# Two heads' attention products in one batch, float32 cluster scores with their split on GpSimd, and a shorter buffer for an early conversion

## The chip, the cores and the metric

The kernel is one launch on one NeuronCore of a Trainium2 chip. The metric is the device time in microseconds (us). The core's engines each run their own instructions in order: TensorE (PE for matmuls, PEld for its weight loads), VectorE (DVE), ScalarE (ACT), GpSimd (POOL) and SyncE (SP), which here only issues DMAs. They meet through semaphores alone.

## The reference

Three layers follow one another: clustered attention (two batches, eight heads, 768 tokens, head width 64, 16 clusters), a mixture of eight experts that sends each of the 1,536 tokens to one expert, and a dense gated layer (512 to 2,048 to 512). The change lies in the attention:

```python
q_assign = np.argmax(np.einsum('bhsd,hcd->bhsc', q_n, c_n), axis=-1)
k_assign = np.argmax(np.einsum('bhsd,hcd->bhsc', k_n, c_n), axis=-1)
mask = q_assign[:, :, :, None] == k_assign[:, :, None, :]
scores = np.where(mask, scale * np.matmul(q, k.transpose(0, 1, 3, 2)), -1000000000.0)
attn = np.exp(scores - np.max(scores, axis=-1, keepdims=True))
attn = attn / (np.sum(attn, axis=-1, keepdims=True) + 1e-09)
return np.matmul(attn, v).astype(np.float32)
```

The weights of the dense layer arrive as 64-bit floats and are turned into 32-bit ones on the chip.

## The kernel before

**Units and steps.** A unit is one batch and a pair of heads; there are eight, u = 0 to 7. A unit has twelve steps, one for each head h and block j of 128 queries, so there are 96 steps, numbered i = 12u + r. In units 0 to 6 all six blocks of head 0 come first, then those of head 1; in unit 7 the order is blocks 0 to 2 of both heads, then blocks 3 to 5 of both.

**One step.** The loop at the end of the attention emits the work by hand, and this sets the order on each engine. In iteration i, `emit_scores(i + 1)` puts four matmuls on PE (L485, L486), which give a row of 768 masked scores, and their row maximum on DVE (L488). `emit_pt(i - 1)` transposes the exponentials of an earlier step on PE (L502), and ACT (L507) and DVE (L509) copy them out of PSUM, half each. `emit_exp(i + 1)` is the exponential on ACT (L494). After three blocks of a head, `queue_av` queues the product with v: 12 matmuls (24 instructions, L525) in groups of 32 output rows, four groups side by side on the array, which sum even and odd key blocks apart; ACT copies the result (`oa`, L528), and two iterations or more later `ostage` multiplies it by `wo` on PE (L540, three 80-column products), which adds the two halves and the router's columns, and DVE scales it (L542).

**Preparing the next unit.** `prep_pieces(u)` holds the pieces of unit u's inputs: transposes of q and k on PE (L318, tile `pqk`), of which ACT writes a rounded high part H (L321) and DVE the rest L (L322); stacks, which are DMAs of H and L into the score operands (L337, on SP); `scores`, eight matmuls of the cluster scores (16 instructions, L392) from H and L; then on DVE a transpose (`by_token`, L396), `argmax_a`, `argmax_b`, `chosen` and `by_cluster` (L400); at last `rows_of_ones`, an ACT operation (`ohT`, L404) and eight small DMAs on SP (L410), which put the mask's rows into `Q2` and `Z`. A list of nine numbers says in which r of the unit before each piece is emitted.

**Early conversion.** Eight tiles of the dense weights are converted during the attention. For each tile `load_early` loads it on SP (L103, L105; two `raw` buffers) and `convert_early`, called from the loop, emits one of four operations: `bits` (a square on ACT, L117, into `csq`, and a DVE operation, L118), `top` (L121), `tail` (L124), and `last`, which is `guard` on DVE (L127, in place in `csq`), a store of `csq` to memory issued on POOL (L163), and the next load. `csq` has two buffers. Calls are at every third iteration from 17 to 83.

**Buffers.** PSUM tile `po` (one buffer) is shared by the product with v and `pqk`; tile `m` (one buffer) by `ostage`, `scores` and the routing. `zero_rows` writes 768 KB of zeros at eight iterations from 14 to 42. After the attention comes the routing, the experts and the dense layer, in which the code is the same before and after.

Of the kernel before, what the change touches and what calls it, by code (L numbers as in the profile page):

```python
# [45 lines left out]
def attention_moe_ffn(ctx: ExitStack, tc: tile.TileContext, q, k, v, centroids, w_gate, w_og, w1, w2, w_in, w_out, out):  # L46
# [87 lines left out]
    pp = at.enter_context(tc.tile_pool(name="pp", reuse_waits="tile", bufs=4))  # L134
    ptp = at.enter_context(tc.tile_pool(name="ptp", reuse_waits="tile", bufs=2))
    xwp = at.enter_context(tc.tile_pool(name="xwp", reuse_waits="tile", bufs=1))
# [17 lines left out]
    def convert_early():  # L154
        if not convert:
            if not ready:
                return
            c, g, t = ready.popleft()
            hold, ops = wide_ops(cva, t)

            def last(f=ops[3]):
                f()
                nc.gpsimd.dma_start(out=wd[2 * c + g // 2][:, (g % 2) * 512:(g % 2) * 512 + 512], in_=hold["s"])  # L163
                load_early()
            convert.extend(ops[:3] + [last])
        convert.popleft()()
# [86 lines left out]
    def setup_rest():  # L253
# [5 lines left out]
        nc.gpsimd.memset(oh_bias[0:64], 0.0)  # L259
        nc.gpsimd.memset(oh_bias[64:128], -BIG)  # L260
        for r in range(2):
            rows = slice(64 * r, 64 * r + 64)
            nc.gpsimd.tensor_copy(wo[rows, :, 0:D], ident[rows, None, rows].to_broadcast([64, H, D]))
            nc.sync.dma_start(out=wo[rows, :, D:D + E], in_=w_gate.rearrange("(h d) e -> d h e", h=H))
            nc.sync.dma_start(out=wo[rows, :, D + E:XW], in_=w_og.rearrange("(h d) e -> d h e", h=H))
        t32 = one.tile([128, 128], F32, name="t32")
# [32 lines left out]
    def prep_pieces(u):  # L299
        d = st[u]  # L300

        def alloc():
            for nm in ("Q1", "X"):
                d[nm] = stk.tile([128, 2, S], F32R, name=nm, tag=nm)
            for nm in ("Q2", "Z"):
                d[nm] = stk.tile([XW, 2, S], F32R, name=nm, tag=nm)
            for nm in ("Hq", "Lq", "Hk", "Lk"):
                d[nm] = one.tile([128, 2, 3 * 128], F32R, name=nm, tag=nm)
            d["sc"] = one.tile([128, 4, T, C], F32, name="sc", tag="sc")

        def transposes(nm, h):
            def f():
# [6 lines left out]
                hi, lo = d["H" + nm][:, h], d["L" + nm][:, h]  # L319
                sc = 0.125 if nm == "q" else 1.0  # L320
                nc.scalar.activation(hi, pt[:, :384], AF.Copy, scale=sc)  # L321
                nc.vector.scalar_tensor_tensor(lo, pt[:, :384], sc, f32(hi), op0=ALU.mult, op1=ALU.subtract)  # L322
# [129 lines left out]
        if u == 0:  # L452
# [13 lines left out]

    steps[-2 * T:] = sorted(steps[-2 * T:], key=lambda s_: s_[2] // 3)
    NS = len(steps)
    live = {}

    def emit_scores(i):
        u, h, j = steps[i]
        d = st[u]
        L = live[i] = {}
        if j % 3 == 0:
            L["sm"] = pp.tile([128, 3], F32, name="sm", tag="sm")
            L["pT"] = ptp.tile([128, T, 384], F32, name="pT", tag="pT")
        else:
            for nm in ("sm", "pT"):
                L[nm] = live[i - 1][nm]  # L480
        sp = L["sp"] = ps_s.tile([128, 2, 512], F32, name="sp", tag="sp")
# [8 lines left out]
    def emit_exp(i):  # L490
        L = live[i]
        j = steps[i][2]
        P = L["P"] = pp.tile([128, 2, 384], F32, name="P", tag="P")
        nc.scalar.activation(P, L["sp"][:, :, :384], AF.Exp, bias=L["nm"], accum_out=L["sm"][:, j % 3:j % 3 + 1])  # L494

    def emit_pt(i):
        L = live[i]
        j = steps[i][2]
        for n in range(2):
# [10 lines left out]
            advance(2)  # L510

    av = deque()
    ost = deque()

    def queue_av(i):
        u, h, j = steps[i]
        L = live[i]
        hold = {}

        def weighted():  # L520
            po = ps_a.tile([128, 512], F32, name="po", tag="po")
            for kt in range(T):
                for a in range(2):
                    g = 2 * (kt % 2) + a
                    nc.tensor.matmul(po[32 * g:32 * g + 32, :384], st[u]["v"][:, h, tile_t(kt), 32 * a:32 * a + 32],  # L525
                                     L["pT"][:, kt, :], start=kt < 2, stop=kt >= T - 2)
            oa = hold["oa"] = pp.tile([128, 384], F32, name="oa", tag="oa")
            nc.scalar.copy(oa, po[:, :384])  # L528
            rs = hold["rs"] = pp.tile([128, 3], F32, name="rs", tag="rs")
            nc.vector.tensor_scalar(rs, L["sm"], 1e-9, None, op0=ALU.add)  # L530
            nc.vector.reciprocal(rs, rs)
            ost.append(ostage)

        def ostage():
            b, pr = UNITS[u]
            hh = 2 * pr + h
            po = ps_m.tile([128, 512], F32, name="pox", tag="m")
            pv = po[:, :3 * XW].rearrange("p (r c) -> p r c", r=3)
            for r in range(3):
                nc.tensor.matmul(pv[:, r], hold["oa"][:, r * 128:(r + 1) * 128], wo[:, hh], start=True, stop=True)  # L540
            j0 = j - 2
            nc.vector.tensor_tensor(xw[b][:, j0:j0 + 3, hh, :], pv, hold["rs"][:, :, None].to_broadcast([128, 3, XW]), op=ALU.mult)  # L542
            if (hh, j0) == (H - 1, 0) and b == B - 1:
                routing.append(route(1))

        av.append(weighted)


# [190 lines left out]
    def prepare(i, early=False):  # L739
        for u, n in plan_at.get((i, early), ()):  # L740
            if u not in pieces:
                pieces[u] = prep_pieces(u)
            for f in pieces[u][n]:
                f()

    with tc.manual_schedule():
# [14 lines left out]
        for i in range(NS + 2):  # L761
# [12 lines left out]
            if i >= 14 and i % 4 == 2 and len(fill) < E:  # L774
                zero_rows(len(fill))
            if i % (NS // 2) == NS // 2 - 5 and i < NS:
                sum_logits(i // (NS // 2))
            if i == NS // 2 + 13:
                routing.append(route(0))
            if i in (9, 12):  # L780
                load_early()
            if i > 16 and i < NS - 12 and i % 3 == 2:
                convert_early()
                if i % 12 != 5:
                    convert_early()
            for _ in range(2 if tail else 1):
                if av:
                    av.popleft()()
            if 0 <= i - 1 < NS:
                emit_pt(i - 1)  # L790
# [12 lines left out]
        advance()  # L803
        finish_routing()
        keep_clock_last(90)
    at.close()
# [481 lines left out]
```

## Time and profile before

| | us |
|---|---|
| median of three runs | 739.1 (737.55 to 740.92) |
| the profiled execution | 738.55 |
| its span, first to last instruction | 736.9 |
| the part from the first exponential (19.1) to the last (261.1) | 242.0 |

| engine | busy us | share of the span |
|---|---|---|
| PE | 713.9 | 97% |
| DVE | 464.3 | 63% |
| ACT | 398.0 | 54% |
| POOL | 223.4 | 30% |

Shares are over the whole span; the attention has its own. Times in the trace are counted from the first instruction. An instruction's shown length runs a little into the next one's (the ends of matmuls are modelled), so the pace of an engine is read from one start to the next.

### The profile page before, as it was taken

The page shows a single profiled execution, that of the slowest core. Times are in us where ns is not written, and L with a number is a line of the kernel's source. Part 1 is how long each engine was busy: PE and PEld are TensorE (multiplying, and loading weights), DVE is VectorE, ACT ScalarE, POOL GpSimd, SP SyncE. Part 2 cuts the span into 40 slices and gives each one's busy share as a digit, 9 for nine tenths or more (in the row PEclk, how much of TensorE's full clock was granted, in tenths as well). Part 3 has the DMA queues.
Part 4 walks back from the last instruction along what each step waited for, and adds up shares of the span by engine and source line. Part 5 has one row for each costly group of instructions (what it writes and reads, how often), then busy time and mean ns, then how long its engine had stood idle before and what let it go on. Part 6 is the DMA issues. An engine that isn't in the chain of part 4 may idle for free.

```text
span 736.9 us, 12871 instructions
## 1 busy us (share of the span) xinstructions
PE 713.9 (97%) x4698; PEld 587.4 (80%) x4698; DVE 464.3 (63%) x918; ACT 398.0 (54%) x792; POOL 223.4 (30%) x165
## 2 busy tenths in 40 slices
PE   8999999999999988999999998999999999999996
PEld 5777777677677767999999898888888888888885
DVE  5979899999978772334455555787555657232322
ACT  7767676767667643555677776535334353222120
POOL 3000000000620034665788888222432212020202
PEclk8999999999999998999999999999999999999999
DMA  6768879658260038665676874234544221010101
GB/s 194 158 183 216 253 234 283 176 137 233 87 179 12 2 133 284 206 203 183 222 231 195 278 238 170 76 104 83 81 58 58 58 78 38 0 58 0 58 1 57
DMA packets 66691, 101.30 MB, mean 137 GB/s; under 512 B 9440, under 2 KB 44384, under 8 KB 66624
## 3 DMA queue, kind: packets, MB, share of 16 engines
q1 hardware_dynamic: 63680, 92.04, 43.9%
q0 software_dynamic: 2944, 8.40, 3.1%
q8 instruction: 38, 0.62, 0.4%
q14 instruction: 29, 0.24, 0.1%
HBM read 66.56 MB, written 14.69 MB: 110 GB/s over the span
## 4 chain that ended last, share of the span: by engine, by line
PE 37%; issue 16%; ACT 3%; DVE 2%; POOL 2%; DMA 0%; POOLq 0%; SPq 0%; ACTq 0%; DVEq 0%
PE ph L1117 4%; PE ph L1116 4%; PE ph L1118 4%; PE py L1209 3%; PE py L1208 3%; PE py L1210 3%; PE py L940 3%; PE ph L940 3%; ACT w L854 2%; PE py L941 1%; PE ph L941 1%; PE ph L936 1%; PE ph L937 1%; PE ph L938 1%; PE py L938 1%
## 5 line engine op out<-in xcount | busy, mean ns | idle before, releaser
L857 POOL TENSOR_TENSOR w<-raw,w 128x1024 fp32r<-128x1024 f32 x51 | 125.4, 2475 | 44.1 <-ACT w L854 27.9
L1193 DVE TENSOR_TENSOR sg<-ph,sg 128x512 f32<-128x512 f32 x48 | 33.2, 691 | 104.5 <-ACT sg L1192 100.4
L488 DVE TENSOR_REDUCE nm<-sp 128x1 f32<-128x768 f32 x96 | 91.3, 952 | 7.8 <-PE sp L486 7.0
L494 ACT ACTIVATE P<-sp,nm 128x768 f32<-128x768 f32 x96 | 87.0, 906 | 6.9 <-DVE nm L488 6.4
L1192 ACT ACTIVATE sg<-ph 128x512 f32<-128x512 f32 x48 | 28.7, 598 | 109.2 <-PE ph L1118 105.9
L502 PEld LDWEIGHTS pt<-ident,P 128*128 128x128 f32 x576 | 65.0, 143 | 23.7 <-issue 19.6
L502 PE MATMUL pt<-ident,P 128*128 128x128 f32 x576 | 82.4, 277 | 1.4 <-DVE pT L509 0.8
L1117 PE MATMUL ph<-ytl,w 128*128 128x512 f32 x192 | 76.1, 396 | 0.0
L1116 PE MATMUL ph<-yth,w 128*128 128x512 f32 x192 | 76.0, 396 | 0.0
L1118 PE MATMUL ph<-yth,w 128*128 128x512 f32 x192 | 75.5, 393 | 0.0
L1209 PE MATMUL py<-w,gh 128*128 128x512 f32 x192 | 75.3, 392 | 0.0
L1208 PE MATMUL py<-w,gh 128*128 128x512 f32 x192 | 74.9, 390 | 0.0
L1210 PE MATMUL py<-w,gl 128*128 128x512 f32 x192 | 74.7, 389 | 0.0
L485 PE MATMUL sp<-X,Q 128*128 128x384 f32 x192 | 73.8, 385 | 0.4 <-ACT P L494 0.4
L854 ACT CAST w<-raw 128x1024 fp32r<-128x1024 f32 x68 | 70.4, 1043 | 3.2 <-DMA raw<-in_moe_w_dram 3.2
L890 POOL TENSOR_TENSOR w<-csq,w 128x512 fp32r<-128x512 f32 x24 | 32.7, 1364 | 120.6 <-ACT w L889 120.6
L525 PE MATMUL po<-pT,ld_v 128*32 128x384 f32 x768 | 68.4, 489 | 0.2 <-ACT pT L507 0.2
L486 PE MATMUL sp<-Z,Q 80*128 80x384 f32 x192 | 65.6, 342 | 0.0
L940 PE MATMUL py<-ht,w 128*128 128x480 f32 (+5 forms) x192 | 61.2, 370 | 3.1 <-DVE ht L964 2.4
L509 DVE COPY pT<-pt 128x384 f32<-128x384 f32 x96 | 52.6, 548 | 15.1 <-PE pt L502 14.5
L940 PE MATMUL ph<-t,w 128*128 128x480 f32 (+5 forms) x192 | 61.3, 371 | 0.0
L163 POOL DMA_DIRECT2D wd<-csq x8 | 4.7, 585 | 163.6 <-DVE csq L127 101.8
(239 smaller groups left out, 1556.8 us busy)
## 6 DMA issues: line engine op xcount, KB each, us to landing
raw<-in_moe_w_dram SPq DMA_DIRECT2D x64, 512.0 KB
raw<-in_moe_w_in_dram SPq DMA_DIRECT2D x16, 512.0 KB
raw<-in_moe_w_out_dram SPq DMA_DIRECT2D x16, 512.0 KB
xd<-zrow SPq DMA_DIRECT2D x8, 768.0 KB
Q<-Hq SPq DMA_DIRECT2D x28, 192.0 KB
ld_q<-in_q_dram SPq DMA_DIRECT2D x8, 384.0 KB
ld_k<-in_k_dram SPq DMA_DIRECT2D x8, 384.0 KB
ld_v<-in_v_dram SPq DMA_DIRECT2D x8, 384.0 KB
```

What stands on the lines that cost most here:

```text
L488: nc.vector.tensor_reduce(nm, sp[:, :, :384], op=ALU.max, axis=AX.XY, negate=True)
L494: nc.scalar.activation(P, L["sp"][:, :, :384], AF.Exp, bias=L["nm"], accum_out=L["sm"][:, j % 3:j % 3 + 1])
L502: nc.tensor.transpose(pt[:, r * 128:(r + 1) * 128], L["P"][:, n, r * 128:(r + 1) * 128], ident)
L854: nc.scalar.copy(hi, r)
L857: (eng or nc.gpsimd).tensor_tensor(lo, r, f32(hi), op=ALU.subtract)
L940: nc.tensor.matmul(ps[:, :2 * n], w_hi, t, start=first, stop=False)
L1116: nc.tensor.matmul(ph, wa(key, 0, k, i), yth[:, k, cs], start=(k == 0), stop=False)
L1117: nc.tensor.matmul(ph, wa(key, 0, k, i), ytl[:, k, cs], start=False, stop=False)
L1118: nc.tensor.matmul(ph, wa(key, 1, k, i), yth[:, k, cs], start=False, stop=(k == 3))
L1208: nc.tensor.matmul(po[m], gh[:, ms], wb(key, 0, i), start=first, stop=False)
L1209: nc.tensor.matmul(po[m], gh[:, ms], wb(key, 1, i), start=False, stop=False)
L1210: nc.tensor.matmul(po[m], gl[:, ms], wb(key, 0, i), start=False, stop=last)
```

## The change

The steps of units 1 to 7 all take the order that unit 7 had. For these units, except the last three blocks of unit 7, the product with v takes both heads at once: 24 matmuls of the same form, two groups of rows for each head, emitted in two parts (key blocks 0 to 2 and 3 to 5) in two iterations one after the other. `oa` then holds head 0 in the upper and head 1 in the lower 64 rows; one `ostage` multiplies it by a block-diagonal `wo` with 160 columns. `pT` has three buffers.

From unit 2 on, ACT writes one float32 copy F of the transposed q and k; POOL makes H from it (a cast) and L (a subtraction), and `scores` uses F: four matmuls instead of eight.

The pieces are emitted at other iterations (`PLAN`), among them `scores` to `argmax_a` at r = 2, behind the product with v, and `rows_of_ones` at r = 9 for r = 8. The conversion's calls stand in a table (`slots`), and `csq` has one buffer.

```diff
-    def wide_ops(pool, t):
+    def wide_ops(pool, t, csq=2):
...
-            hold["s"] = pool.tile([128, 512], F32, name="csq", tag="csq", bufs=2)
+            hold["s"] = pool.tile([128, 512], F32, name="csq", tag="csq", bufs=csq)
...
-            hold, ops = wide_ops(cva, t)
+            hold, ops = wide_ops(cva, t, 1)
...
-    wo = one.tile([128, H, XW], F32, name="wo")
+    wo = one.tile([128, H // 2, 2, XW], F32, name="wo")
+    wl = one.tile([128, H, XW], F32, name="wl")
...
+                if u > 1:
+                    full = d["F" + nm][:, h]
+                    nc.scalar.activation(full, pt[:, :384], AF.Copy, scale=sc)
+                    nc.gpsimd.tensor_copy(hi, full)
+                    nc.gpsimd.tensor_tensor(lo, full, f32(hi), op=ALU.subtract)
+                    return
...
-            for n, x in enumerate("HL"):
-                for g in range(4):
-                    nm, h = "qk"[g // 2], g % 2
-                    nc.tensor.matmul(d["cl"][32 * g:32 * g + 32, :384], cfull[:, 2 * pr + h], f32(d[x + nm][:, h]),
-                                     start=n == 0, stop=n == 1)
+            for g in range(4):
+                nm, h = "qk"[g // 2], g % 2
+                parts = [f32(d[x + nm][:, h]) for x in ("HL" if u == 1 else "F")]
+                for n, x in enumerate(parts):
+                    nc.tensor.matmul(d["cl"][32 * g:32 * g + 32, :384], cfull[:, 2 * pr + h], x, start=n == 0, stop=n == len(parts) - 1)
...
-            [], [scores, by_token, argmax_a], [argmax_b], [chosen], [by_cluster, rows_of_ones],
+            [], [scores, by_token, argmax_a], [argmax_b], [chosen], [by_cluster], [rows_of_ones],
...
-    steps[-2 * T:] = sorted(steps[-2 * T:], key=lambda s_: s_[2] // 3)
+    steps[2 * T:] = sorted(steps[2 * T:], key=lambda s_: (s_[0], s_[2] // 3))
...
+    KTS = (range(0, 3), range(3, T))
...
+        alone = u == 0 or i >= NS - T
+        heads = (h,) if alone else (0, 1)
...
+            for kt in kts:
+                for n, hh in enumerate(heads):
+                    for a in range(2):
+                        g = 2 * (kt % 2 if alone else n) + a
+                        nc.tensor.matmul(po[32 * g:32 * g + 32, :384], v_[:, hh, tile_t(kt), 32 * a:32 * a + 32],
+                                         pts[n][:, kt, :], start=kt < (2 if alone else 1), stop=kt >= T - (2 if alone else 1))
...
+                nc.tensor.matmul(pv[:, r], hold["oa"][:, r * 128:(r + 1) * 128], wl[:, 2 * pr + h] if alone else wo[:, pr], start=True, stop=True)
...
+    PLAN = ((0, 0, 0, 1, 3, 5, 6, 7, 8, 8), (-3, -2, 0, 1, 1, 2, 3, 8, 8, 9), (-2, -1, 0, 1, 1, 2, 3, 8, 8, 9))
...
-        for n, r in enumerate((-3, -2, 0, 1, 3, 5, 6, 7, 8) if u > 1 else (0, 0, 0, 1, 3, 5, 6, 7, 8)):
-            plan_at.setdefault((12 * (u - 1) + r, n == 6), []).append((u, n))
+        for n, r in enumerate(PLAN[min(u, 3) - 1]):
+            plan_at.setdefault((12 * (u - 1) + r, n == 6, n == 5 and u > 1), []).append((u, n))
...
+    slots = {12 * u + r: n for u in range(1, 5) for r, n in ((3, 1), (8, 1), (9, 2))}
+    slots.update({11: 2, 68: 1, 69: 1, 75: 1, 80: 2, 81: 2, 86: 2, 87: 2, 92: 1, 93: 2})
...
-            if i in (9, 12):
+            if i in (8, 11):
                 load_early()
-            if i > 16 and i < NS - 12 and i % 3 == 2:
+            for _ in range(slots.get(i, 0)):
                 convert_early()
-                if i % 12 != 5:
-                    convert_early()
```

## Rows read from the trace of the kernel before

**Rows 1.** Busy time by stretch, units 1, 3, 5: length, engines (instructions), clock, DMA.
```profile
47.07:77.64 30.57, 30.57 (x270) 22.80 (x269) 27.22 (x53) 21.69 (x49) 0.78 (x1) 1.00 0.82 216
...
108.72:140.87 32.15, 31.00 (x270) 22.76 (x269) 29.61 (x56) 21.63 (x49) 0.90 (x2) 1.00 0.77 224
...
171.72:204.62 32.90, 31.75 (x276) 22.91 (x275) 31.20 (x74) 21.43 (x49) 14.00 (x12) 1.00 0.59 161
```
**Rows 2.** Timeline of unit 7: start us, us, engine, line, operation, tiles, count.
```profile
234.97 0.79 PE L540 MATMUL pox<-wo,oa 128*128 128x80 f32 x6
...
235.60 0.82 PE L502 MATMUL pt<-ident,P 128*128 128x128 f32 x6
...
236.12 0.48 ACT L507 COPY pT<-pt 128x384 f32<-128x384 f32 x1 [0.63 <-PE pt L502]
...
237.56 0.48 ACT L507 COPY pT<-pt 128x384 f32<-128x384 f32 x1
...
238.44 2.14 PE L525 MATMUL po<-pT,ld_v 128*32 128x384 f32 x24
...
240.52 0.87 PE L502 MATMUL pt<-ident,P 128*128 128x128 f32 x6
...
241.95 0.79 PE L540 MATMUL pox<-wo,oa 128*128 128x80 f32 x6
```
**Rows 3.** Timeline of PE at the cluster scores of unit 4.
```profile
120.31 0.52 PE L392 MATMUL pcl<-Hq,cfull 128*32 128x384 f32 x2
...
121.62 2.12 PE L525 MATMUL po<-pT,ld_v 128*32 128x384 f32 x24
```
**Rows 4.** Timeline of ACT at two steps that also transpose q.
```profile
134.85 0.50 ACT L321 ACTIVATE Hq<-pqk 128x384 fp32r<-128x384 f32 x1
...
136.58 0.49 ACT L321 ACTIVATE Hq<-pqk 128x384 fp32r<-128x384 f32 x1
```
**Rows 5.** Groups by line up to 330 us: busy us, mean ns, idle before and releasers.
```profile
L857 POOL TENSOR_TENSOR w<-raw,w 128x1024 fp32r<-128x1024 f32 x13 | 31.1, 2411 | 24.1 <-DMA raw<-in_moe_w_dram 10.6 <-ACT w L854 8.7 <-PE ph L938 2.6
...
L857 DVE TENSOR_TENSOR w<-raw,w 128x1024 fp32r<-128x1024 f32 x5 | 6.9, 1396 | 4.3 <-ACT w L854 4.3
...
L404 ACT ACTIVATE ohT<-oT,oh_bias,oh_scale 128x384 fp32r<-128x384 bf16 x7 | 5.0, 708 | 10.4 <-DVE oT L400 7.8 <-issue 1.3 <-DVE rs L530 1.3
...
L368 DVE TENSOR_TENSOR eq<-eq,rev 128x384 f32<-128x384 f32 x7 | 3.9, 559 | 0.2
```
**Rows 6.** Timeline around one store of the conversion.
```profile
131.80 0.64 DVE L127 SCALAR_TENSOR_TENSOR csq<-csq,ct 128x512 f32<-128x512 f32 x1
...
132.52 0.66 ACT L117 ACTIVATE csq<-raw 128x512 f32<-128x512 f32 x1
...
132.73 0.54 POOL L163 DMA_DIRECT2D wd<-csq  x1 [23.66 <-DVE csq L127]
```
**Rows 7.** DMA packets of POOL's queue from 133.8 to 135.0: count, MB, share.
```profile
q0 software_dynamic: 80, 0.26, 58.3%
```
**Rows 8.** Timeline of POOL: another store of the conversion.
```profile
147.59 0.54 POOL L163 DMA_DIRECT2D wd<-csq  x1 [14.31 <-DVE csq L127]
```
**Rows 9.** DMA packets by queue from 149.4 to 153.1: count, MB, share.
```profile
q1 hardware_dynamic: 561, 0.76, 83.5%
q0 software_dynamic: 80, 0.26, 21.8%
```
**Rows 10.** Timeline of SP's DMA issues in unit 0.
```profile
43.23 1.22 SPq L410 DMA_DIRECT2D Q<-ohT  x2
...
46.15 0.46 SPq L103 DMA_DIRECT2D raw<-in_moe_w_in_dram  x1
```
**Rows 11.** Timeline of ACT at iteration 11.
```profile
46.25 0.48 ACT L528 COPY oa<-po 128x384 f32<-128x384 f32 x1 [1.68 <-PE po L525]
```
**Rows 12.** Timeline of unit 5: DVE and POOL at work together.
```profile
195.40 1.97 POOL L651 TENSOR_SCALAR xs<-xw,gate 128x512 f32<-128x512 f32 x1
...
195.97 1.07 DVE L124 SCALAR_TENSOR_TENSOR ct<-raw,ct 128x512 int32<-128x512 int32 x1
```

More of the change, by code (lines that the diff above doesn't have):

```diff
@@ L260, in setup_rest @@
         nc.gpsimd.memset(oh_bias[64:128], -BIG)
+        nc.gpsimd.memset(wo, 0.0)
         for r in range(2):
             rows = slice(64 * r, 64 * r + 64)
-            nc.gpsimd.tensor_copy(wo[rows, :, 0:D], ident[rows, None, rows].to_broadcast([64, H, D]))
-            nc.sync.dma_start(out=wo[rows, :, D:D + E], in_=w_gate.rearrange("(h d) e -> d h e", h=H))
-            nc.sync.dma_start(out=wo[rows, :, D + E:XW], in_=w_og.rearrange("(h d) e -> d h e", h=H))
+            nc.gpsimd.tensor_copy(wl[rows, :, 0:D], ident[rows, None, rows].to_broadcast([64, H, D]))
+            nc.sync.dma_start(out=wl[rows, :, D:D + E], in_=w_gate.rearrange("(h d) e -> d h e", h=H))
+            nc.sync.dma_start(out=wl[rows, :, D + E:XW], in_=w_og.rearrange("(h d) e -> d h e", h=H))
+            nc.gpsimd.tensor_copy(wo[rows, :, r, :], wl[rows].rearrange("p (x r) c -> p x r c", r=2)[:, :, r])
         t32 = one.tile([128, 128], F32, name="t32")
@@ L308, in alloc @@
                 d[nm] = one.tile([128, 2, 3 * 128], F32R, name=nm, tag=nm)
+            if u > 1:
+                for nm in ("Fq", "Fk"):
+                    d[nm] = one.tile([128, 2, 3 * 128], F32, name=nm, tag=nm)
             d["sc"] = one.tile([128, 4, T, C], F32, name="sc", tag="sc")
@@ L474, in emit_scores @@
         L = live[i] = {}
+        L["sm"] = live[i - 1]["sm"] if i % (6 if u else 3) else pp.tile([128, 2, 3], F32, name="sm", tag="sm")
         if j % 3 == 0:
-            L["sm"] = pp.tile([128, 3], F32, name="sm", tag="sm")
             L["pT"] = ptp.tile([128, T, 384], F32, name="pT", tag="pT")
         else:
-            for nm in ("sm", "pT"):
-                L[nm] = live[i - 1][nm]
+            L["pT"] = live[i - 1]["pT"]
         sp = L["sp"] = ps_s.tile([128, 2, 512], F32, name="sp", tag="sp")
@@ L516, in queue_av @@
         u, h, j = steps[i]
-        L = live[i]
-        hold = {}
-        def weighted():
[L521 to L531, printed above, removed]
+        b, pr = UNITS[u]
@@ new lines, in queue_av, with products @@
+        v_ = st[u]["v"]
+        j0 = j - 2
+        alone = u == 0 or i >= NS - T
+        heads = (h,) if alone else (0, 1)
+        if len(heads) == 2 and h == 0:
+            return
+        pts = [live[i]["pT"]] if alone else [live[i - 3]["pT"], live[i]["pT"]]
+        sums = live[i]["sm"]
+        hold = {}
+        def products(kts):
+            if "po" not in hold:
+                hold["po"] = ps_a.tile([128, 512], F32, name="po", tag="po")
+            po = hold["po"]
+            for kt in kts:
[4 more added lines that the diff above has]
+                                         pts[n][:, kt, :], start=kt < (2 if alone else 1), stop=kt >= T - (2 if alone else 1))
@@ L532, in weighted @@
+        def weighted():
+            products(KTS[-1] if not alone else range(T))
+            oa = hold["oa"] = pp.tile([128, 384], F32, name="oa", tag="oa", bufs=2)
+            nc.scalar.copy(oa, hold["po"][:, :384])
+            rs = hold["rs"] = pp.tile([128, 2, 3], F32, name="rs", tag="rs")
+            hs = slice(heads[0], heads[-1] + 1)
+            nc.vector.tensor_scalar(rs[:, hs], sums[:, hs], 1e-9, None, op0=ALU.add)
+            nc.vector.reciprocal(rs[:, hs], rs[:, hs])
             ost.append(ostage)
@@ L534, in ostage @@
         def ostage():
-            b, pr = UNITS[u]
-            hh = 2 * pr + h
+            n = len(heads)
+            hh = 2 * pr + heads[0]
             po = ps_m.tile([128, 512], F32, name="pox", tag="m")
-            pv = po[:, :3 * XW].rearrange("p (r c) -> p r c", r=3)
+            pv = po[:, :3 * n * XW].rearrange("p (r h c) -> p r h c", r=3, h=n)
             for r in range(3):
-                nc.tensor.matmul(pv[:, r], hold["oa"][:, r * 128:(r + 1) * 128], wo[:, hh], start=True, stop=True)
@@ L541, in ostage @@
-            j0 = j - 2
-            nc.vector.tensor_tensor(xw[b][:, j0:j0 + 3, hh, :], pv, hold["rs"][:, :, None].to_broadcast([128, 3, XW]), op=ALU.mult)
-            if (hh, j0) == (H - 1, 0) and b == B - 1:
+                nc.tensor.matmul(pv[:, r], hold["oa"][:, r * 128:(r + 1) * 128], wl[:, 2 * pr + h] if alone else wo[:, pr], start=True, stop=True)
+            scale = hold["rs"][:, heads[0]:heads[-1] + 1].rearrange("p h r -> p r h")
+            nc.vector.tensor_tensor(xw[b][:, j0:j0 + 3, hh:hh + n, :], pv, scale[:, :, :, None].to_broadcast([128, 3, n, XW]), op=ALU.mult)
@@ L544, in ostage @@
+            if (pr, j0) == (H // 2 - 1, 0) and b == B - 1:
                 routing.append(route(1))
+        if not alone:
+            for kts in KTS[:-1]:
+                av.append(lambda kts=kts: products(kts))
         av.append(weighted)
@@ L730, in place_ids, with prepare @@
             nc.vector.tensor_tensor(ci[:, b], t2, place[b], op=ALU.add)
+    PLAN = ((0, 0, 0, 1, 3, 5, 6, 7, 8, 8), (-3, -2, 0, 1, 1, 2, 3, 8, 8, 9), (-2, -1, 0, 1, 1, 2, 3, 8, 8, 9))
     plan_at = {}
     for u in range(1, len(UNITS)):
-        for n, r in enumerate((-3, -2, 0, 1, 3, 5, 6, 7, 8) if u > 1 else (0, 0, 0, 1, 3, 5, 6, 7, 8)):
-            plan_at.setdefault((12 * (u - 1) + r, n == 6), []).append((u, n))
+        for n, r in enumerate(PLAN[min(u, 3) - 1]):
+            plan_at.setdefault((12 * (u - 1) + r, n == 6, n == 5 and u > 1), []).append((u, n))
     pieces = {}
-    def prepare(i, early=False):
-        for u, n in plan_at.get((i, early), ()):
+    def prepare(i, early=False, late=False):
+        for u, n in plan_at.get((i, early, late), ()):
             if u not in pieces:
@@ L775, in attention_moe_ffn @@
                 zero_rows(len(fill))
-            if i % (NS // 2) == NS // 2 - 5 and i < NS:
+            if i % (NS // 2) == NS // 2 - 4 and i < NS:
                 sum_logits(i // (NS // 2))
@@ L804, in attention_moe_ffn @@
         finish_routing()
+        assert not (early or ready or convert)
         keep_clock_last(90)
```

8 lines of the change are left out of this document (5 added, 3 removed).

## The prediction, as put on record before the changed kernel was seen

> **What bounds the kernel now.** I read the busy time by stretch first, cut at every twelfth exponential, one stretch a unit [rows 1]. A clean unit is 30.57 us and PE is busy for all of it, at the full 2.4 GHz; in units 3 and 5, which take 32.15 and 32.90, PE idles for only 1.15 of each. DVE is busy 27 to 31 us of a unit, so it is nearly a second bound; ACT has a third of its time free, but in some steps only. The timeline of unit 7, which prepares nothing, gives the pieces [rows 2]: three steps take 6.98 us (234.97 to 241.95), of which `ostage` 0.63, the product with v 2.08 (238.44 to 240.52), and the rest, 4.27, is 1.42 for scores and transposes of one step. ACT needs 1.44 for a bare step (one copy to the next). So a bare step leaves nothing on ACT, and a step with the product leaves it about 2 us. Experts and dense layer have the same code; I count nothing there. The sum is made against the profiled 738.55 (span 736.9 and 1.65 around it), 0.55 under the median.
>
> **What PE saves.** (a) `ostage`. Two heads cost 2 x 0.63 now. Sixteen score instructions of 384 columns, four at a time, take 1.31 [rows 3], so 384 columns stream in 0.33 and 160 in 0.14: six instructions are 0.82. Thirteen pairs save 13 x 0.44 = 5.7. Bounds: 0 if 160 columns cost twice 80, 8.2 if they cost the same. (b) Cluster scores: half of 1.31 for units 2 to 7 is 6 x 0.66 = 3.9. (c) The product with v keeps its matmuls and their form: 0. (d) `rows_of_ones` one iteration later no longer makes ACT wait for DVE's `by_cluster`; that wait was 7.8 us in sum [rows 5], mostly under the product with v. I count 2.0, from the idle PE of units 3 and 5 [rows 1], between 0 and 4.
>
> **What is late next.** (e) `scores` now stands behind the first product with v. Its four DVE operations at about 0.56 [rows 5], and `argmax_b` in the next step, start about 3.8 us after their step does, where before they ran under the product. DVE's copy of `pT` waits behind them, the transposes of two steps later wait for that copy's PSUM buffer, and no product comes at r = 4 to cover it: I work out 0.9 a unit, 6 x 0.9 = 5.4, between 0 and 8. (f) `rows_of_ones` at r = 9 issues eight DMAs, 0.61 each [rows 10], and unit u + 1 needs the first four at r = 11: issued about 4.5 us after step r = 9 begins, needed at 5.4, with a landing in between. I count 0.3 for six units, 1.8, between 0 and 1 each. (g) POOL: a cast and a subtraction of 384 columns. A 1,024-column subtraction took 2.41 [rows 5], so 0.9 each at most, 1.8 for the pair against 1.73 for a step that transposes [rows 4]. Four such steps stand in a row; POOL ends under a step late, and only stacks and their DMAs wait, with eight steps to spare: 0. DVE's saved L (24 x 0.55) comes in steps that PE or ACT bound: 0, up to 2 gained. ACT's copy F is as long as H was: 0. The third `pT` buffer removes a wait that the batch would else make: 0. Building `wo` is POOL work at the start, when POOL is idle: 0.
>
> Base: -5.7 - 3.9 - 2.0 + 5.4 + 1.8 = -4.4.
>
> **The conversion's new waits.** With one `csq`, the square of a tile must wait until the store of the tile before has landed, and ACT is in order: `oa`, the copy of `pT` and the exponential stand behind it, and PE waits for all three. Before, with two, the square was emitted beside the store and waited for nothing [rows 6]. A store takes POOL 0.3 to begin after `guard`, and its last packet comes at most 2.3 us after the issue (132.73 to 135.0) on quiet queues [rows 6, 7]; with stacks and loads in flight it was up to 5.5 (147.59 to 153.1) [rows 8, 9]. How long the landing takes after the last packet no row shows; I take 0.3, little above nothing, since the spread between the two stores is far larger: 2.9 to 6.1 us from `guard` to the square.
>
> (h) At i = 81 and 87 the table puts `guard` and the next square into one iteration. `guard` ends about 2.6 us into the step (scores, maximum, `guard`), so the square ends at 2.6 + 2.9 + 0.7 = 6.2. `oa` would have begun at 3.2 or so (scores 0.8, product 2.1, the way to ACT). Loss about 2.8, twice: 5.6, between 4 and 12. (i) At i = 21, 33, 45 and 57 `guard` is at r = 8 and the square at r = 9. Here `guard` ends 3.5 into r = 8, just as r = 9 begins; the square ends 3.6 after that when the store is quick, `oa` would begin at 3.2: loss 0.4; with a slow store 3.7. At 57 no zeros are written, so I take 0.5. At 21, 33 and 45 zeros, a load of 0.5 MB and the loads of a unit, now ahead of the rows in SP's order, are just draining; nearer to the quick end, 1.5 each. In sum 5.0, between 1.6 and 13. A lengthened r = 9 gives the rows of (f) time to land: -1.2. (j) At i = 11 the first square follows its load, issued three iterations before but behind the eight row DMAs of unit 1, thus at 44.45, where it was at 46.15 for a square at i = 17 [rows 10]. A load has twice the bytes of a store: about 3.5 us, landing at 48.0; square until 48.7; `oa` began at 46.25 [rows 11]. Loss 2.4, between 1.5 and 3.5.
>
> Sum: -4.4 + 5.6 + 5.0 - 1.2 + 2.4 = +7.4. Against the median, less what two waits at one place share, I forecast 745.5 us.
>
> **A rule on the stores.** The trace's stores take from 2.3 to 5.5 us to their last packet [rows 6 to 9]. The Trainium skill ("DMA: Bandwidth & Descriptors", section "Anatomy of one DMA — SWDGE (gpsimd) path") gives about 2.0 us fixed, mostly the receipt after the last byte, and bytes over 436e3: an estimate of 2.6 us for 256 KB. By that (i) would be 4 x 0.4 and the sum about +4. The trace agrees on quiet queues alone.
>
> **Rivals.** First, quick stores throughout: (i) 1.6 and (h) 4.5, with (j) 1.5 and (e) 4: -5.7 - 3.9 - 2.0 + 4 + 1.8 + 1.6 + 4.5 - 1.2 + 1.5 = +0.6, so 739 to 742, no change that can be told. For it: at r = 8 no stacks are in flight. Against: the same-iteration waits of (h) are there however quick the store.
>
> Second, and faster: the squares' waits are covered. The place is r = 9 and 3, where ACT has 2 us free under the product; if DVE's `guard` runs early enough that the store lands before the second product ends, (h) shrinks to 2 and (i) to 0, and with (j) at 1.5 the sum is -4.4 + 2 + 1.5 = -0.9; if (e) is covered too, -6.3, so 732 to 738. It decides at a store under about 1 us from `guard` at i = 81, or a `guard` 2 us earlier. Against: `guard` stands behind the row maximum of its own step, and the quickest store seen leaves no packet before 133.8.
>
> Third, slow stores at all six places: -4.4 + 10 + 11 + 2.4 - 1.2 = +18, so 757. Against: the slow ones had a stack's DMAs beside them [rows 9], which r = 8 and 9 don't.
>
> Fourth, POOL slows DVE. One DVE operation with two SBUF inputs took 1.07 beside a POOL operation, itself 1.97 long [rows 12]; the like beside none, `guard`, took 0.64 [rows 6]. If all 24 pairs of POOL each met one such operation it would be 24 x 0.4 = 10 us more. But POOL's new work falls at r = 10, 11, 0 and 1, and the operations with two SBUF inputs at r = 2, 3, 8 and 9; the maximum and the copies there read PSUM. I take 0. The Trainium skill ("GPSIMD Engine Reference", sections 1 and 4.1) says that both share their SBUF interfaces, that DVE operations with two SBUF inputs are met, and that elementwise work on two inputs belongs on VectorE. The trace agrees on the first where they meet, and on the second by 2.41 against 1.40 [rows 5]; by it the change would be slower by that other way.
>
> **How the numbers follow.** A difference under 0.5% (3.7 us) can hardly be told from no change here; 742.8 and 735.4 are the bounds. The forecast (stores near the quick end but not all, 743 to 750) has 0.50; quick stores, 739 to 742, 0.20; covered waits, 732 to 738, 0.18, of which a third is within 0.5%; slow stores or a slowed DVE, 750 to 760, 0.12. So slower 0.62, the same 0.25, faster 0.13. The range leaves out the lowest tenth and the highest: 735 to 753. The forecast's own case reaches from 743 to 750.
>
> **What would show it.** In the changed profile: `ostage`'s six 160-column instructions in 0.8, and eight score instructions in 0.66 (a, b). ACT idle before the conversion's square, released by the DMA of the store, some 2 to 3 us at i = 81 and 87 and 0.5 to 3 at 21, 33, 45 and 57, PE idle just after; idle before the first square, released by its load (h, i, j). PE waiting for the copy of `pT` at r = 4 (e), and for the rows at the start of a unit, under 1 us (f). No wait for POOL (g). The units without conversion waits near 29.5 us. The prediction is wrong if the square does not wait, if the product covers it, or if (e) is far from 0.9.

## The result, and the profile after

The changed kernel is slower: 747.2 us, median of six executions (743.59 to 748.29), against 739.1 (737.55 to 740.92) for six of the kernel before; the ratio is 1.0097, with an interval of 1.0081 to 1.0112. The forecast was 745.5, in a range of 735 to 753. The profiled execution of the changed kernel took 743.59 (span 741.6), the lowest of its six, against 738.55 before. So the traces can explain 5.0 us between the two profiled executions, and not the whole 8.1 between the medians.

Where the 5.0 arose: the attention, from its first exponential (18.32) to its last (263.93), takes 245.6, 3.6 more than before. It begins 0.8 earlier; routing and what follows up to the first expert cost 0.7 more; the rest lies in the experts and around the span. Busy time by stretch, units 1, 3, 5, 6 and 7 (length, then PE, PEld, DVE, ACT, POOL, granted clock, DMA share, GB/s), to be read beside [rows 1]:

```profile
48.74:78.59 29.85, 27.43 (x223) 20.28 (x223) 24.52 (x43) 19.74 (x46) 5.46 (x8) 1.00 0.89 252
...
108.11:138.68 30.57, 29.93 (x251) 21.78 (x250) 25.88 (x43) 19.83 (x46) 6.59 (x10) 1.00 0.77 227
...
168.41:198.78 30.37, 29.57 (x255) 21.75 (x254) 27.32 (x60) 19.76 (x47) 16.54 (x16) 1.00 0.44 114
198.78:232.29 33.51, 30.59 (x243) 21.92 (x242) 26.10 (x42) 19.81 (x44) 12.00 (x13) 0.95 0.53 147
232.29:263.93 31.64, 29.56 (x252) 20.53 (x251) 24.16 (x42) 17.11 (x39) 1.11 (x2) 1.00 0.05 18
```

Units 6 and 7 of the kernel before, in the same columns:

```profile
204.62:234.50 29.88, 29.88 (x264) 22.31 (x263) 24.09 (x46) 19.85 (x44) 3.18 (x3) 1.00 0.41 107
234.50:261.08 26.58, 26.58 (x233) 19.87 (x232) 20.10 (x42) 17.23 (x38) 0.00 (x0) 1.00 0.00 1
```

Units 1 to 5 are shorter than before, but PE is no longer busy for all of a unit. Unit 6 is 3.6 longer and unit 7 is 5.1 longer, 3.0 of it because PE has more to do there: five products with v fall into it, where four did. Over the whole attention PE is busy 4.6 us less than before (234.06 against 238.70) and idle 8.3 more (11.55 against 3.26): the change gave PE less to do, and something made it wait.

The groups by line (busy us, mean ns, idle before and what ended it) name the engine that carries the wait. Line 117 is the conversion's square on ACT; the first row is that of the kernel before, the others are those of the changed kernel. The rows of POOL's cast and subtraction and of `ohT` are to be read beside [rows 4, 5]:

```profile
L117 ACT ACTIVATE csq<-raw 128x512 f32<-128x512 f32 x8 | 5.4, 678 | 0.0
```

```profile
L331 POOL TENSOR_TENSOR Lq<-Fq,Hq 128x384 fp32r<-128x384 f32 x12 | 12.0, 1002 | 1.0
...
L330 POOL CAST Hq<-Fq 128x384 fp32r<-128x384 f32 x12 | 6.1, 506 | 33.2 <-DMA Z<-ohT 12.9 <-ACT Fq L329 10.7 <-DMA Q<-ohT 9.2
...
L117 ACT ACTIVATE csq<-raw 128x512 f32<-128x512 f32 x8 | 5.4, 672 | 17.3 <-DVE rs L558 4.3 <-DVE pT L520 4.0 <-DMA raw<-in_moe_w_in_dram 3.7
...
L416 ACT ACTIVATE ohT<-oT,oh_bias,oh_scale 128x384 fp32r<-128x384 bf16 x7 | 4.9, 705 | 1.3 <-issue 1.3
```

The wait of `ohT` for DVE's `by_cluster` is gone (7.8 before, nothing after). ACT's idle time before the square is 17.3 where it was 0.0, put down mostly to DVE and to the load. Neither `rs` nor `pT` feeds a square. The timeline around i = 81 shows what ACT waits for (start, us, engine, line; it is to be read beside [rows 6], `ostage` beside [rows 2]). The first and the last exponential in it bound the step:

```profile
222.02 0.91 ACT L505 ACTIVATE P<-sp,nm 128x768 f32<-128x768 f32 x1
...
223.75 0.68 DVE L127 SCALAR_TENSOR_TENSOR csq<-csq,ct 128x512 f32<-128x512 f32 x1
...
224.73 0.60 POOL L163 DMA_DIRECT2D wd<-csq  x1 [13.59 <-DVE csq L127]
...
227.20 0.66 ACT L117 ACTIVATE csq<-raw 128x512 f32<-128x512 f32 x1 [3.58 <-issue]
227.76 0.46 ACT L554 COPY oa<-po 128x384 f32<-128x384 f32 x1
228.12 0.48 ACT L518 COPY pT<-pt 128x384 f32<-128x384 f32 x1
228.49 0.92 ACT L505 ACTIVATE P<-sp,nm 128x768 f32<-128x768 f32 x1
...
228.66 0.71 PE L513 MATMUL pt<-ident,P 128*128 128x128 f32 x3 [1.93 <-ACT pT L518]
...
233.01 0.98 PE L567 MATMUL pox<-wo,oa 128*128 128x160 f32 x6
...
233.83 0.38 PE L513 MATMUL pt<-ident,P 128*128 128x128 f32 x2
```

`guard` ends at 224.43, POOL issues the store at 224.73, and the square that writes the same buffer starts at 227.20, 2.77 after `guard`. The list of DMAs in this stretch gives the store's landing, 2.4 after its issue (KB, us to landing):

```profile
wd<-csq POOLq DMA_DIRECT2D x1, 256.0 KB, 2.4
```

So the square starts when the store has landed. `oa`, the copy of `pT` and the exponential stand behind it on ACT, and PE idles 1.93. At the six places where a square follows a store in the same or the next iteration, the time from `guard`'s end to the square is 4.18 (i = 21), 2.76, 2.72, 2.68, 2.77 and 2.69 (i = 87); the forecast had 2.9 for a quick store. `ostage` takes 0.82 to the next matmul (233.01 to 233.83), as forecast.

At i = 11 the square waits for its load (SP's issue, ACT, PE; to be read beside [rows 10, 11]):

```profile
43.59 0.58 SPq L103 DMA_DIRECT2D raw<-in_moe_w_in_dram  x1
...
47.44 0.67 ACT L117 ACTIVATE csq<-raw 128x512 f32<-128x512 f32 x1 [3.68 <-DMA raw<-in_moe_w_in_dram]
...
48.01 0.47 ACT L554 COPY oa<-po 128x384 f32<-128x384 f32 x1
...
48.53 0.90 PE L567 MATMUL pox<-wl,oa 128*128 128x80 f32 x6 [1.61 <-ACT oa L554]
```

The load is used 3.85 after its issue (forecast 3.5, issue forecast at 44.45, seen at 43.59).

In steps, from one exponential to the next, i = 11 takes 5.99 (3.50 before); i = 21, 33, 45 and 57 take 5.23, 3.83, 4.83 and 3.75, where the same step without a wait (i = 69) takes 3.58; i = 81 and 87 take 6.47 and 6.27. The waits make these seven steps 2.5 + 3.3 + 5.6 = 11.4 us longer. That is not what they cost the attention: a step just behind a wait is often shorter than without it (i = 82 takes 1.25 here and 1.78 in the run with two buffers below), and some are longer at a lower clock. What the attention takes without the waits is measured below: 237.2 and 237.5, so 8.2 to 8.4 less than here and 4.5 to 4.8 less than before.

### The profile page after: what moved, and what is told of

Same layout as the page of the kernel before. It is cut to its first block, busy times and chain, and to the rows that moved or that the text cites. A ratio compares the mean times of both kernels' runs of the same rounds, so it can differ in the third digit from the quotient of the medians.

```text
span 741.6 us, 12556 instructions
## 1 busy us (share of the span) xinstructions
PE 709.2 (96%) x4572; PEld 582.0 (78%) x4572; DVE 453.8 (61%) x855; ACT 390.2 (53%) x779; POOL 262.1 (35%) x216
## 4 chain that ended last, share of the span: by engine, by line
PE 59%; issue 18%; DVE 11%; ACT 6%; POOL 2%; DMA 2%; SPq 1%; POOLq 0%; ACTq 0%; DVEq 0%
PE pt L513 6%; PE po L548 6%; PE sp L496 4%; PE ph L1151 4%; PE ph L1150 4%; PE ph L1152 4%; PE sp L497 3%; PE py L1243 3%; PE py L1242 3%; PE py L1244 3%; ACT w L888 3%; PE py L974 2%; PE ph L974 2%; PE pox L567 2%; DVE nm L499 1%
## 5 line engine op out<-in xcount | busy, mean ns | idle before, releaser
L513 PE MATMUL pt<-ident,P 128*128 128x128 f32 x576 | 84.4, 279 | 8.0 <-ACT pT L518 5.5
L518 ACT COPY pT<-pt 128x384 f32<-128x384 f32 x96 | 46.1, 480 | 37.5 <-PE pt L513 37.3
```

What stands on the lines that cost most here:

```text
L513: nc.tensor.transpose(pt[:, r * 128:(r + 1) * 128], L["P"][:, n, r * 128:(r + 1) * 128], ident)
```

## The experiments

All ratios are to the kernel before, with its own runs on the same chip beside them; the attention's length and the steps are read from one trace of each run. The theory throughout: the waits of the squares for `csq` and for the first load make the change slower, and the new product and scores are by themselves faster.

**Two buffers again.** The changed kernel with two `csq`; the buffer count of `P` makes the room.

```diff
-            hold, ops = wide_ops(cva, t, 1)
+            hold, ops = wide_ops(cva, t, 2)
-        P = L["P"] = pp.tile([128, 2, 384], F32, name="P", tag="P")
+        P = L["P"] = pp.tile([128, 2, 384], F32, name="P", tag="P", bufs=3)
```

> The changed kernel with two csq buffers again, room made by three P buffers for four (a fourth is not needed: an exponential's P is read one iteration later). Theory (the square waits in ACT's order for the store of the tile before): the steps with a square at i = 21, 33, 45, 57, 81 and 87, which took 5.23, 3.83, 4.83, 3.75, 6.47 and 6.27 us from one exponential to the next, fall to about 3.6; 8.8 us in all, so a ratio to the kernel before of 0.996 to 0.999 for 1.0097. Rival 1 (what costs is the new order of the steps and DVE's work behind the scores, and the store's wait is covered by the product with v): the six steps and the ratio stay, 1.008 to 1.011. Rival 2 (the single buffer delays, but the time is made up by the next steps, which get faster): the six steps fall, the ratio by less than half of 8.8 us, 1.004 or more.

Measured: 0.996 (0.9943 to 0.9978), 737.26 us. The six steps fall to 3.58 or 3.59, all of them; i = 11 stays at 6.12, and the square's group has only the load's wait left:

```profile
L117 ACT ACTIVATE csq<-raw 128x512 f32<-128x512 f32 x8 | 5.6, 697 | 3.8 <-DMA raw<-in_moe_w_in_dram 3.8
```

In the timeline of this run at i = 81 the square, emitted beside the store, waits for nothing:

```profile
224.70 0.70 ACT L117 ACTIVATE csq<-raw 128x512 f32<-128x512 f32 x1
224.94 0.68 DVE L127 SCALAR_TENSOR_TENSOR csq<-csq,ct 128x512 f32<-128x512 f32 x1
...
225.92 0.60 POOL L163 DMA_DIRECT2D wd<-csq  x1 [13.65 <-DVE csq L127]
225.99 0.48 ACT L554 COPY oa<-po 128x384 f32<-128x384 f32 x1 [0.59 <-PE po L548]
```

So the single buffer alone turns the change from a gain into a loss. In its trace the attention is 240.95, only 4.7 shorter than in the changed kernel's, though the six steps together lose 8.9: unit 1 grew from 29.85 to 31.55 although its own long step (i = 21) is gone, and the granted clock there was 0.50 from 49.5 to 52.7 and from 63.2 to 66.4.

**One buffer, square and store apart.** The table of calls is shifted so that at least five iterations lie between a store and the next square; one `csq`.

```diff
-    slots.update({11: 2, 68: 1, 69: 1, 75: 1, 80: 2, 81: 2, 86: 2, 87: 2, 92: 1, 93: 2})
+    slots.update({11: 3, 68: 1, 75: 2, 80: 1, 81: 1, 86: 2, 87: 2, 92: 2, 93: 2})
```

> The changed kernel, still one csq buffer, with the calls of the conversion shifted by one operation, so that every square comes five steps or more after the store before it (table: three calls at 11, one at 68, two at 75, one at 80 and 81, two at 86, 87, 92 and 93). No buffer is added. Theory (waiting for the store): the same gain as two buffers give, the steps at 81 and 87 near 3.6 us, ratio 0.996 to 1.000; iteration 11 gets 0.7 us more of DVE. Rival (DVE's work at those steps costs, not the buffer): steps 81 and 87 still hold a square and two or three DVE operations and stay over 5 us, ratio 1.006 or more.

Measured: 0.9978 (0.9964 to 0.9991), 738.18 us; steps 81 and 87 at 3.58 and 3.59, and 3.59 or 3.60 at the other four. It is the nearness of store and square that costs, not the number of buffers; a second buffer is one way to relax it. The distance is only just enough, though: two of the squares still wait, 0.26 and 0.22, without a longer step. The stores before them landed 6.9 and 7.8 after their issue; they now run beside loads of the next unit. POOL's issue and the square, the store's landing, and the DMA packets from 94.1 to 102.1:

```profile
94.23 0.59 POOL L163 DMA_DIRECT2D wd<-csq  x1 [7.02 <-DVE rs L558]
...
102.07 0.71 ACT L117 ACTIVATE csq<-raw 128x512 f32<-128x512 f32 x1 [0.22 <-DMA wd<-csq]
```

```profile
q1 hardware_dynamic: 1141, 2.36, 91.7%
...
wd<-csq POOLq DMA_DIRECT2D x1, 256.0 KB, 7.8
```

**The first load earlier.** Only the load of the first tile moves, ahead of the row DMAs of unit 1.

```diff
-            if i in (8, 11):
+            if i in (7, 11):
```

> The changed kernel with the first tile's load emitted at iteration 7 for 8, so that it stands ahead of the eight row DMAs of unit 1 in SP's order. Theory (at i = 11 ACT's square and DVE wait for that load): the step i = 11 falls from 5.99 to 3.5 us, nothing else moves, 2.5 us, ratio 1.006 to 1.007. Rival (the step is long because a square and two DVE operations were put there): it stays above 5 us, ratio 1.009 to 1.011.

Measured: 1.0036 (1.0022 to 1.0051), 742.71 us; i = 11 falls from 5.99 to 3.94. So the load's wait is shown, but the rest of the expectation missed. The median fell by 4.5 and not by 2.5, and other steps did move: in the trace i = 21 takes 4.07 for 5.23, and i = 12, 17 and 18 together 1.9 more, with a stretch at the lower clock in unit 1 (0.69 from 62 to 66 in the mean). The attention of this one trace is only 1.1 shorter; where the median's other 3.4 lie, stays open.

**The kernel before with one buffer.** The opposite test: the old attention, old table, one `csq`.

```diff
-            hold, ops = wide_ops(cva, t)
+            hold, ops = wide_ops(cva, t, 1)
```

> The kernel before with one csq buffer, nothing else. Its calls put guard and the next square into one iteration at i = 23, 44 and 50, and three iterations apart elsewhere. Theory: three long steps; stores at these places landed 3 to 8 us after guard in the trace of before, and the square starts after that; 3 to 7 us each, 10 to 18 in all, ratio 1.013 to 1.025. Rival (one buffer is harmless, the new order of the steps is what costs): ratio 0.998 to 1.003.

Measured: 1.028 (1.0263 to 1.0297), 759.95 us, a little above what was expected. Three steps grow: i = 23, 44 and 50 take 9.84, 8.17 and 7.97, where they took 3.50, 5.24 and 3.50; 13.7 in sum. In this run's timeline at i = 23 `guard` ends at 75.58 and the square starts 6.3 later, when the store has landed, 5.9 after its issue:

```profile
75.90 0.78 POOL L163 DMA_DIRECT2D wd<-csq  x1 [62.74 <-DVE csq L127]
...
81.84 0.66 ACT L117 ACTIVATE csq<-raw 128x512 f32<-128x512 f32 x1 [7.56 <-issue]
82.40 0.46 ACT L528 COPY oa<-po 128x384 f32<-128x384 f32 x1
...
82.91 0.50 PE L540 MATMUL pox<-wo,oa 128*128 128x80 f32 x1 [5.50 <-ACT oa L528]
```

```profile
wd<-csq POOLq DMA_DIRECT2D x1, 256.0 KB, 5.9
```

The DMA packets by queue between 75.9 and 81.8 (count, MB, share of the 16 engines) show the company that the store had:

```profile
q1 hardware_dynamic: 1150, 1.63, 90.6%
q0 software_dynamic: 80, 0.26, 12.8%
```

In the changed kernel, between 224.7 and 227.2 at i = 81, the same 80 packets of the store were nearly alone:

```profile
q0 software_dynamic: 80, 0.26, 28.7%
q1 hardware_dynamic: 128, 0.10, 16.6%
```

From POOL's issue to the square it is 5.94 here and 2.47 there. The Trainium skill ("DMA: Bandwidth & Descriptors", section "Anatomy of one DMA — SWDGE (gpsimd) path") gives the estimate of 2.6 that stands in the prediction; the quiet case agrees with it, and the case with 1.63 MB beside it does not. The other 6.4 us by which the attention grew lie in the steps behind the long ones (after i = 23: 3.05, 3.25 and 3.74 for 2.37, 1.76 and 3.50), and there the granted clock was 0.50, the lower of the two levels, 1.2 GHz. Busy time from 82.6 to 89.2, in the columns of the stretches above:

```profile
82.60:89.20 6.60, 6.29 (x28) 6.19 (x29) 2.80 (x5) 4.04 (x10) 0.00 (x0) 0.50 0.84 261
```

**Both waits taken away, with two buffers.** The first edit above, with its buffer count of `P`, and the earlier load together.

```diff
-            hold, ops = wide_ops(cva, t, 1)
+            hold, ops = wide_ops(cva, t, 2)
...
-            if i in (8, 11):
+            if i in (7, 11):
```

> The changed kernel without both waits: two csq buffers (three P buffers make room) and the first tile's load at iteration 7. Theory: the two gains add, so the step i = 11 falls to about 3.6 as the six others did, 2.5 us under the version with two buffers alone, and no long step is left for the half clock to follow: ratio to the kernel before 0.991 to 0.994. Rival (with the six waits gone the first one is partly made up in unit 1): 0.995 to 0.997.

Measured: 0.9924 (0.9898 to 0.9949), 735.12 us; attention 237.21. The step i = 11, expected at 3.6, is still 4.69, now in part because of what was passed: PE waits for rows of unit 1, issued on SP behind the load (timeline of PE in this run; in the run with the earlier load alone the same wait was 0.17):

```profile
45.14 0.41 PE L497 MATMUL sp<-Z,Q 80*128 80x384 f32 x1 [0.96 <-DMA Q<-ohT]
```

**Both waits taken away, with one buffer.** The shifted table and the earlier load.

```diff
-    slots.update({11: 2, 68: 1, 69: 1, ...})
+    slots.update({11: 3, 68: 1, 75: 2, ...})
...
-            if i in (8, 11):
+            if i in (7, 11):
```

> One csq buffer, the shifted table of calls, and the first load at iteration 7: both waits gone without any more memory. Theory: as the first within 0.2%, ratio 0.991 to 0.995; the third operation at i = 11 costs up to 0.5 us. Rival (with one buffer some other wait stays): 0.996 or more.

Measured: 0.9924 (0.9902 to 0.9947), 734.63 us; attention 237.45, with i = 11 at 4.85. The same as with two buffers.

**Cluster scores ahead of the product.** On top of the run with both waits gone and two buffers, `scores` goes back in front of the first product with v.

```diff
-            plan_at.setdefault((12 * (u - 1) + r, n == 6, n == 5 and u > 1), []).append((u, n))
+            plan_at.setdefault((12 * (u - 1) + r, n == 6, False), []).append((u, n))
```

> As the one before, with the cluster scores at r = 2 ahead of the product with v, where the change put them behind it. The prediction's step (e): behind the product DVE's four operations end too late and the step r = 4 has 0.9 us of PE waiting; the traces show r = 4 at 2.0 against 1.5 for r = 5, so 0.5 a unit, six units. Theory: r = 4 falls to about 1.5 and the time by 2 to 3 us, ratio 0.988 to 0.991. Rival (what DVE is spared at r = 4 it lacks elsewhere: by its sum of work in r = 2 to 4 the place of the scores does not matter): r = 2 gets longer or r = 4 stays, ratio as without.

Measured: 0.9875 (0.9841 to 0.991), 731.51 us, just below what was expected; r = 4 stops at 1.79, where 1.5 was expected. In units 2 to 4 step r = 4 falls from about 2.05 to 1.79 and r = 5 from 1.52 to 1.40; in unit 1 r = 3 falls from 3.42 to 2.00, in unit 6 from 4.40 to 3.58. Units 1 to 6 together give back 3.6.

**The old split.** The run with both waits gone and two buffers, with H on ACT, L on DVE and eight score matmuls in all units; nothing on POOL.

```diff
-            if u > 1:
+            if False:
...
-                parts = [f32(d[x + nm][:, h]) for x in ("HL" if u == 1 else "F")]
+                parts = [f32(d[x + nm][:, h]) for x in "HL"]
```

> As the first, with the old split in all units: H on ACT from PSUM, L on DVE, eight matmuls for the cluster scores, no F and nothing new on GpSimd. Theory: PE loses 0.66 us in the step of the scores (r = 2) and DVE gets 0.55 more in the four steps that transpose, where PE or ACT set the pace; 4 to 6 us in all, ratio 0.997 to 1.000. Rival (GpSimd's share slows DVE, or brings nothing): the same ratio as the first, or lower.

Measured: 0.9981 (0.9963 to 0.9999), 739.48 us; r = 2 takes 4.84 for 4.14, 4.1 in the six units, and the attention is 3.5 longer. So float32 scores with POOL's split are worth 3.5, and POOL's part costs less than they save. It does cost something in one place: r = 3 of unit 6 falls from 4.40 to 3.59 with the old split, the scores still behind the product. What POOL does there is shown in the last section.

**`ostage` in 80 columns.** The run with the scores ahead, with twelve instructions a pair for six.

```diff
-                nc.tensor.matmul(pv[:, r], ..., wl[:, 2 * pr + h] if alone else wo[:, pr], start=True, stop=True)
+                for x in range(n):
+                    nc.tensor.matmul(pv[:, r, x], ..., wl[:, 2 * pr + h] if alone else wo[:, pr, x], start=True, stop=True)
```

> As the version with two csq buffers, the first load at 7 and the scores ahead (ratio 0.9875), but a pair's result is multiplied by 80 columns at a time, twelve instructions for the six of 160 columns. Term (a) of the prediction: six of 80 columns took 0.63 us, six of 160 are 0.82, so a pair costs 1.26 again and thirteen pairs lose 13 x 0.44 = 5.7 us: ratio 0.994 to 0.997. Rival (the steps with ostage, r = 0 and 6, are bound by ACT or DVE, and PE's saving there is idle): under 2 us, ratio 0.987 to 0.990.

Measured: 0.9967 (0.9953 to 0.9982), 737.39 us, where the run with the scores ahead had 0.9875 (by the ratios some 6.8 us, on another chip); the attention is 5.5 longer. PE's timeline of the two runs at one pair, first with 80 columns, then with 160:

```profile
107.31 1.46 PE L568 MATMUL pox<-wo,oa 128*128 128x80 f32 x12
```

```profile
106.48 0.98 PE L567 MATMUL pox<-wo,oa 128*128 128x160 f32 x6
```

**The version that follows.** The shifted table, the load at i = 7 and the scores ahead, with one `csq` and no buffer added.

```diff
-            plan_at.setdefault((12 * (u - 1) + r, n == 6, n == 5 and u > 1), []).append((u, n))
+            plan_at.setdefault((12 * (u - 1) + r, n == 6, False), []).append((u, n))
...
-    slots.update({11: 2, 68: 1, 69: 1, ...})
+    slots.update({11: 3, 68: 1, 75: 2, ...})
...
-            if i in (8, 11):
+            if i in (7, 11):
```

> One csq buffer and no buffer more than the change has: the shifted table of calls, the first load at 7, the scores ahead of the product. Theory: the same as with two buffers, ratio 0.985 to 0.990. Rival (the scores ahead need the room that the second buffer gives the conversion): 0.992 or more.

Measured: 0.9883 (0.9866 to 0.9901), 731.08 us; attention 232.97, in which PE idles 2.8. It beats both kernels, as the other run with the scores ahead does.

## Why the prediction was right

The direction, the place and the mechanism held. The size came out near in part by luck, as the end of this section shows. The terms, in the prediction's letters:

- **(h), forecast 5.6:** 5.6. Steps 81 and 87 lost 2.9 and 2.7; the store was quick and the loss came all the same. The run with two buffers and the run with the shifted table both bring these steps to 3.58 or 3.59.
- **(j), forecast 2.4:** 2.5. With the earlier load alone 0.4 of it is left; in the two runs without the other waits 1.2 and 1.35 are left.
- **(i), forecast 5.0:** 3.3. Here the term was mis-sized. Three of the four stores were quick (2.68 to 2.76 to the square), only the one at i = 21 took 4.18. At i = 45 it was not the store that was late: `guard` ended 0.8 into the step, where at 33 it ended 0.25 before it.
- **(a), forecast 5.7:** 5.5 by the run with 80 columns.
- **(b), forecast 3.9:** 4.1, by r = 2 of the six units in the run with the old split.
- **(g), forecast 0:** a loss of 0.8. POOL's pair takes 0.51 + 1.00, so the bound of 0.9 for the subtraction was too low. No engine waited for POOL, but in unit 6 it slowed DVE, and r = 3 there is 0.8 shorter with the old split (4.40 and 3.59). The fourth rival has this mechanism; it was given nothing, because POOL's work was put at r = 10 to 1. In unit 6 it stood behind POOL's work for the routing and ran at r = 1 to 3.
- **(d), forecast 2.0:** the wait is gone from the trace; its price was not tried by itself, and the sum below leaves nothing for it.
- **(e), forecast 5.4:** 3.6 by the run with the scores ahead, of which 0.8 is the same step r = 3 of unit 6, which either edit shortens; 2.8 without it. It is not where it was put: units 2 to 5 lose only 0.1 to 0.5 each, and unit 1 loses 1.5, nearly all at r = 3, where unit 1 has no product with v to cover it.
- **(f), forecast 1.8:** nothing that shows (1.62 for the step at r = 11 in units 1 to 4), and so nothing to be got back of it at r = 9 either, where the sum had 1.2; a wait for rows came only when a load was put ahead of them in SP's order, in unit 1.

The base, forecast as -4.4, was about -5.9. This is read from the two runs without the waits: their attention, with what is left in i = 11 taken off, is 237.2 - 1.2 and 237.5 - 1.35, against 242.0 before. The terms as measured give the same without (d): -5.5 - 4.1 + 0.8 + 2.8 = -6.0, if they add up. The waits cost the attention 9.5 net, where the sum had 11.8: the seven steps are 11.4 longer, and 1.9 of it is made up in other steps. So the attention lost 3.6 where 7.4 was forecast. Of the 3.8 between them the base explains 1.5, (i) 1.7, and the steps that make up 0.7 (1.9 for the 1.2 of the rows).

The last step of the prediction, from +7.4 to 745.5, takes 1.0 off for waits that share a place and gives no working for it. That the forecast lies within 2 us of the median is luck to this extent: what the attention lost less was made up by what the prediction counted as nothing. Outside the attention the profiled execution lost 1.4 more; the experts' start shows one such place, with the granted clock at 0.50 from 283.5 to 293.7, where before it was so from 280.9 to 287.7. The remaining 3 between the medians lie in executions without a trace. Their mean granted clock was 0.976 to 0.981, against 0.983 in the profiled one, so more time at the lower level is likely; which stretches, stays open.

Of the rivals, quick stores was right about the stores at five of the six places and wrong about the waits: the steps grew by 11.4, where it had 1.6 + 4.5 + 1.5 = 7.6. Covered waits fell: each of the six squares made its step longer, if by as little as 0.2. Slow stores fell for this kernel and is what the kernel before shows when it has one buffer, with 1.63 MB of other DMAs beside the store at i = 23. POOL slowing DVE came true in one unit of six, for 0.8 and not 10 us.

## What to carry to other kernels

A buffer that a DMA empties is free only when its store has landed, and an engine that works in order holds up everything behind the first instruction that needs the buffer; before taking a buffer away, look at what is emitted between the store's issue and the next write, and put at least the landing time there, read for the traffic that the store will meet: here it was 2.4 us beside little and 5.9 to 7.8 beside 1.6 to 2.6 MB. Moving a few calls in the table and one load did as much as the second buffer, and no memory was needed. When a change bundles several edits, cost the waits and the savings each by itself: in the attention 4.5 to 4.8 us of gain were hidden under 8.2 to 8.4 of waits. And a wait's price is not the length that its step gains: of 11.4 us so gained some was made up behind the waits.

## What was not expected of the hardware

**The lower clock behind a wait.** After PE's idle 1.93 at i = 81 the granted clock was 0.50, 1.2 GHz, from 228.9 to 232.3 (the changed kernel's busy time, columns as above):

```profile
229.00:232.20 3.20, 3.02 (x13) 2.56 (x11) 1.46 (x2) 2.09 (x6) 0.00 (x0) 0.50 0.50 172
```

Six transposes there take 1.47, where they take 0.82 at the full clock. Over all runs ten steps were longer than 5.9 us, each with PE idle in it; with seven of them a stretch at 0.50 began within 1.6 us of the step's end. In the six experiments whose steps were all shorter than that, the attention had none. It is no strict rule: one of the changed kernel's three long steps had such a stretch behind it, and two runs had a stretch near 62 us without a long step.

**DVE and POOL at once.** In unit 6 of the changed kernel POOL came late to the split, behind its work for the routing (L681 and the DMA of its result):

```profile
201.41 0.52 POOL L330 CAST Hq<-Fq 128x384 fp32r<-128x384 f32 x1
...
203.00 1.57 POOL L681 TENSOR_SCALAR xs<-xw,gate 128x512 f32<-128x512 f32 x1
```

Two DVE operations with two SBUF inputs then met POOL's cast and subtraction, at r = 3:

```profile
207.49 0.50 POOL L330 CAST Hk<-Fk 128x384 fp32r<-128x384 f32 x1
207.56 0.84 DVE L379 TENSOR_TENSOR eq<-sc,m 128x384 f32<-128x384 f32 x1
208.07 1.21 POOL L331 TENSOR_TENSOR Lk<-Fk,Hk 128x384 fp32r<-128x384 f32 x1
208.44 1.25 DVE L380 TENSOR_TENSOR eq<-eq,rev 128x384 f32<-128x384 f32 x1
```

In the other units both take 0.56 on DVE, and r = 3 takes 3.58 or 3.59 in units 2 to 4, where it takes 4.33 here. The Trainium skill ("GPSIMD Engine Reference", section 1) has the rule that GpSimd shares its SBUF interfaces with VectorE, whose operations with two SBUF inputs are met; this meeting agrees, and it came once in the six units that use the new split.

**The name on a wait.** A wait for a buffer that a store empties was named after DVE's `rs`, DVE's `pT` or "issue" in 11.9 of the 13.7 us before the squares that follow a store; the DMA was named for 1.8. The last event before the instruction is taken, and only the buffer's history showed which wait it was.
